# One product of sums for both halves of a pair, and an earlier list for the second pair, in an attention and MoE kernel

## Chip, cores and metric

The kernel runs on one core of a Trainium2 chip. The metric is device time in microseconds (us), the median of the runs; lower is better. Three runs of the kernel before gave 986.38, 987.79 and 989.44 us; the profiled execution has a span of 986.2 us.

## The reference

Routed attention, then a feed-forward block. Each query and each key is assigned to the nearest of 16 centroids of its head; a query sees only the keys of its own cluster.

```python
# q, k, v: (4, 8, 768, 64); centroids: (8, 16, 64)
mask = q_assign[:, :, :, None] == k_assign[:, :, None, :]
scores = where(mask, scale * (q @ k.T), -1e9)
attn = exp(scores - max); attn = attn / (sum(attn) + 1e-9)
x = (attn @ v) as (3072, 512)
h = x @ w_in                      # 512 x 2048
out = (h - tanh(h)) @ w_out       # 2048 x 512
```

## The kernel before

The 32 heads are taken as 16 pairs of heads: pair `n` is batch `n // 4`, heads `2 * (n % 4)` and the one after. The 768 queries of a pair are taken in two halves of 384. One half of one pair takes three steps of two key chunks each. The first batch runs all first halves of its four pairs and then all second halves (steps 0 to 23); every later pair runs half 0 and then half 1, six steps in a row.

In a step TensorE makes the scores of the step that follows (`begin`, line 451), with keys on the partitions, and the values product of the present step (`value`, line 505); ScalarE takes the exponential (473). VectorE multiplies it by the mask (`select`, line 483: row code equals key code) for each of the two key chunks and two heads, four operations a step. For most halves GpSimd adds the masked exponentials over the chunks into a tile `sum` (lines 492 and 496), so that only one product with ones is left at the end of a half: `total`, lines 532 to 553. It makes two products of 64 columns (line 539), one for each head, and ScalarE copies them out (544). For the first halves of the first batch TensorE accumulates the sums itself in four products of 32 columns a step (`sum_up`, line 520).

What follows depends on the pair. Where the result is needed soon (`soon(n)`: the last pair of each batch, and pair 2), VectorE takes reciprocals of the whole tile (603) and scales `xT` (606). Otherwise the sums travel by memory, since each is repeated on 64 partitions: `total` writes one row of each head to a list in DRAM (553), `compact` reads the list back spread over 128 partitions, six numbers each (566), `invert` takes the reciprocal on VectorE (575) and writes it back (577), `spread_out` reads it broadcast to 64 partitions a head (582), and `scale` multiplies (588). These five stages are put in `later` at 0, 1, 2, 3 and 5 steps after the end of the half; for pair 1's first half the last three come a step later (`slow`, line 1110).

Beside the attention steps runs the feed-forward block of the batch before: plain products for the first batch (lines 626 and 642), and for the others a Strassen form with 7 products in place of 8 (`up_product`, line 818, and `down_product`, line 869). `strassen_items` and `plain_items` return pieces with a weight, and each step takes as many as are due. Inside a piece `between()` is called; it takes the next share of the list `todo`, whose entry `i` of `len(todo)` falls into slot `i * slots / len(todo)`. So the length of `todo` decides how late each entry is issued. All engines run in the order that this program writes. Buffers: two of `sum` and two of `den` in pool `sump`, two score tiles in PSUM (`ps_s`, also used by the transposes of line 332), and three tiles of `ps_f` for everything else.

Of the kernel before, what the change touches and what calls it, by code (L numbers as in the profile page):

```python
# [30 lines left out]
F32 = mybir.dt.float32  # L31
# [4 lines left out]
ALU = mybir.AluOpType  # L36
# [22 lines left out]
def kernel(  # L59
# [119 lines left out]
    def fast():  # L179
# [352 lines left out]
        def total(n: int, half: int):  # L532
# [17 lines left out]
            for i in range(parts):  # L550
                for h in range(2):
                    r = h * D + i * D // 2
                    nc.sync.dma_start(lists[n, half][i, h : h + 1], t[r : r + 1])

        lists, spots = {}, {}
# [2 lines left out]
            return pairs[n][1] == HP - 1 or n == HP - 2  # L560

        def compact(n: int, half: int):
            spots[n, half] = each[:, len(spots)]
            t = lists.pop((n, half))
            for i in range(t.shape[0]):
                nc.sync.dma_start(
                    other if i else spots[n, half],
                    t[i].rearrange("h n -> (h n)").rearrange("(p i) -> p i", p=P),
                )

        def invert(n: int, half: int):
            t = spots[n, half]
            if summed(n, half):
                nc.vector.tensor_tensor(out=t, in0=t, in1=other, op=ALU.add)
            nc.vector.reciprocal(out=t, in_=t)
            back = lists[n, half] = dram.tile([2, TB], F32, name="back")
            nc.sync.dma_start(back.rearrange("h n -> (h n)").rearrange("(p i) -> p i", p=P), t)

        def spread_out(n: int, half: int):
            back = lists.pop((n, half))  # L580
            for h in range(2):
                nc.sync.dma_start(
                    dens[n, half][h * D : h * D + D], back[h : h + 1].to_broadcast([D, TB])
                )

        def scale(n: int, half: int):
            x = xT[n][:, half]
            nc.vector.tensor_tensor(out=x, in0=x, in1=dens.pop((n, half)), op=ALU.mult)

        tallies, picks = {}, []  # L590

# [157 lines left out]
        def open_stream():  # L749
            first_in.close()  # L750
            late_pools["stream"] = cx.enter_context(
                tc.tile_pool(name="stream_late", bufs=3, side="right", reuse_waits="tile")
            )
            for n in range(2):
                fetch_factors(n)
# [294 lines left out]
        for at, (n, half, s) in enumerate(steps):  # L1050
            b, p = pairs[n]
            following = steps[at + 1] if at + 1 < len(steps) else None
            if at == 4 * HALF:
                open_late()
            if at == 4 * HALF - 9:
                open_stream()
            if at in fills:
                fill, over = fills[at][0](), fills[at][1]
                whole, spent, since = sum(it[0] for it in fill), 0.0, at
            if at == 2 * HALF:  # L1060
                makers = [it for i in range(2) for it in up_maker(i)]
                makers += [it for i in range(2) for it in down_maker(i)]
            now = []
            part = (at - since + 1) / over
            while fill and (spent + fill[0][0] / 2 <= whole * part or part == 1):
                now.append(fill.pop(0))
                spent += now[-1][0]
            stages = ready.get(at, {})

            values_first = 1 in stages and not summed(n, half)  # L1070
            if values_first:
                value(n, half, s)
            if 1 in stages:
                stages[1]()

            for ahead, known in ((2, False), (5, True)):
                to = steps[at + ahead] if at + ahead < len(steps) else None
                if to and to[2] == 0 and (to[0] < HP and to[1] == 1) == known:
                    if not masked(*to[:2]):
                        spread(*to[:2])  # L1080
            if following and at >= NS - 1:
                begin(following)
            while picks:
                picks.pop(0)()
            share = paces.get(at, 0)
            todays, rounding = rounding[:share], rounding[share:]
            taken = s == NS - 1 and summed(n, half)
            if not taken:
                for piece in todays[:2]:
                    rest_of(piece)  # L1090
            if not values_first:
                value(n, half, s)
            if summed(n, half):
                if 0 in stages:
                    stages.pop(0)()
                sum_up(n, half, s)
            if s == NS - 1:
                take(n, half)
                if taken:
                    if soon(n):  # L1100
                        total(n, half)
                    for piece in todays[:2]:
                        rest_of(piece)
                if soon(n):
                    if summed(n, half):
                        picks.append(lambda n=n, half=half: pick(n, half))
                    divides = [lambda n=n, half=half, i=i: divide(n, half, i) for i in range(HCH)]
                else:

                    slow = int((n, half) == (1, 0))  # L1110
                    for i, stage in (
                        (0, total), (1, compact), (2 + slow, invert), (3 + slow, spread_out),
                        (5 + slow, scale),
                    ):
                        later.setdefault(at + i, []).append(
                            (i, lambda stage=stage, n=n, half=half: stage(n, half))
                        )

                if p == HP - 1 and (half == 1 or b == 0):
                    if summed(n, half):  # L1120
                        picks += divides
                    else:
                        total(n, half)
                        late += divides
                    divides = []
                if (n, half) == (HP - 1, 0):
                    load(HP)
                if half == 1:
                    load(n + (HP if n < 2 else 2), (2,) if n < 2 or n >= HP else ())

            todo = []
            if following:
                todo += [lambda i=i: select(*following[:2], 2 * following[2] + i) for i in range(2)]
            todo += [stages[i] for i in (5, 3, 4, 2) if i in stages]
            todo += late
            late = []
            if divides:
                if not taken:
                    todo.append(lambda n=n, half=half: total(n, half))
                late, divides = divides, []  # L1140

            for it in later.pop(at, []):
                if it[0] == 0:
                    todo.append(it[1])
                else:
                    listed.append(it[1])
            for i, piece in enumerate(todays):
                todo.append(lambda piece=piece: round_piece(piece))
                if i == 0:
                    todo += [lambda piece=piece: rest_of(piece) for piece in todays[2:]]  # L1150
            todo += listed
            listed = []

            light = [i for i in range(at, 4 * HALF - 2) if i % 3 and i % 6 != 1]
            if makers and at in light:
                share = -(-len(makers) // len(light))
                todo += makers[:share]
                del makers[:share]
            if "raw" in late_pools:
                todo += [check_done, check_done, check_on, check_on]  # L1160
                if p == HP - 1 and half == 1 and s == NS - 2:
                    todo += [lambda b=b, c=c: right_factors(b, c) for c in range(CH - 1)]
            slots = max(sum(it[1] for it in now), 1)
            place = iter(range(slots))
            turned_at = max(slots - 1 - now[-1][1], 0) if now else 0

            def between():
                i = next(place)
                for it in todo[i * len(todo) // slots : (i + 1) * len(todo) // slots]:
                    it()  # L1170

                if i == turned_at and 0 in stages:
                    stages[0]()

            if at in fills and "raw" in late_pools:
                for c in range(CH - 1 if at > 4 * HALF else 0, CH):
                    right_factors(b - 1, c)
            for it in now:
                it[2](between)
            if not now:  # L1180
                between()
# [225 lines left out]
```

## Time and profile before

| view | value |
|---|---|
| time, median of 3 | 987.79 us |
| span of the profiled execution | 986.2 us |
| line 539, products of the sums | 112 records, 22.8 us busy |
| line 520, the same with 32 columns | 96 records, 10.2 us busy |
| line 544, copy of a sum | 32, 491 ns each |
| line 496, add to a sum on GpSimd | 112, 1841 ns each |
| line 575, reciprocal of a list | 22, 184 ns each |
| line 588, scale | 22, mean 974 ns, median 556 ns |
| HBM traffic | 133 GB/s over the span |

A product in float32 appears in the trace as two records of TensorE, so one `total` is four records. A record is shown with its full latency (486 ns for 384 columns of moving data) while the next has long begun, so times of one record can't be added: the distance between starts is what TensorE spends. The chain of the page is followed back from the last instruction, and names at each step the work that released it.

### The profile page before, as it was taken

The page shows a single profiled execution, that of the slowest core. Times are in us where ns is not written, and L with a number is a line of the kernel's source. Part 1 is how long each engine was busy: PE and PEld are TensorE (multiplying, and loading weights), DVE is VectorE, ACT ScalarE, POOL GpSimd, SP SyncE. Part 2 cuts the span into 40 slices and gives each one's busy share as a digit, 9 for nine tenths or more (in the row PEclk, how much of TensorE's full clock was granted, in tenths as well). Part 3 has the DMA queues.
Part 4 walks back from the last instruction along what each step waited for, and adds up shares of the span by engine and source line. Part 5 has one row for each costly group of instructions (what it writes and reads, how often), then busy time and mean ns, then how long its engine had stood idle before and what let it go on. Part 6 is the DMA issues. An engine that isn't in the chain of part 4 may idle for free.

```text
span 986.2 us, 16627 instructions
## 1 busy us (share of the span) xinstructions
PE 976.0 (99%) x6456; PEld 464.9 (47%) x6456; DVE 531.0 (54%) x1019; ACT 321.5 (33%) x493; POOL 499.7 (51%) x347
## 2 busy tenths in 40 slices
PE   9999999999999999999999999999999999999997
PEld 5433443344443334444455555444455555444664
DVE  6457756447656567647554356655645336543011
ACT  5575554233333333243322222333341221122000
POOL 1025334445445454687676345666688345466600
PEclk9999999999999999999999999999999999999999
DMA  8755452025474723463635636344453232233221
GB/s 205 179 162 163 150 145 94 30 52 153 127 224 136 216 99 118 148 196 96 192 106 193 198 114 213 110 152 121 151 165 110 85 110 81 96 113 127 105 102 35
DMA packets 115977, 132.47 MB, mean 134 GB/s; under 512 B 62980, under 2 KB 95668, under 8 KB 113204
## 3 DMA queue, kind: packets, MB, share of 16 engines
q1 hardware_dynamic: 109508, 109.81, 37.0%
q0 software_dynamic: 6240, 21.50, 6.5%
q8 instruction: 53, 0.87, 0.4%
q14 instruction: 32, 0.26, 0.1%
q10 hardware_dynamic: 144, 0.03, 0.0%
HBM read 110.14 MB, written 21.17 MB: 133 GB/s over the span
## 4 chain that ended last, share of the span: by engine, by line
PE 94%; DVE 2%; DMA 2%; issue 1%; ACT 1%; SPq 0%; ACTq 0%; DVEq 0%
PE pd L869 22%; PE pu L818 22%; PE sc L451 13%; PE av L505 13%; PE o L642 8%; PE h L626 8%; PE pt L332 2%; PE den L539 2%; PE sim L351 1%; DMA den<-back 1%; PE pr L364 1%; DVE e L483 1%; PE den L520 0%; DMA back<-each 0%; PE pq L396 0%
## 5 line engine op out<-in xcount | busy, mean ns | idle before, releaser
L496 POOL TENSOR_TENSOR sum<-sum,e 128x768 f32<-128x768 f32 x112 | 206.2, 1841 | 105.2 <-DVE e L483 101.4
L483 DVE SCALAR_TENSOR_TENSOR e<-row,code,sc 128x384 f32<-128x384 bf16 x336 | 185.3, 608 | 94.9 <-ACT sc L473 72.1
L473 ACT ACTIVATE sc<-sc 128x768 f32<-128x768 f32 x168 | 125.9, 792 | 205.3 <-PE sc L451 187.6
L869 PE MATMUL pd<-stream,G 128*64 128x256 f32 x1728 | 191.8, 379 | 0.0
L869 PEld LDWEIGHTS pd<-stream,G 128*64 128x64 f32 x1728 | 123.7, 137 | 67.4 <-issue 7.9
L451 PE MATMUL sc<-t,t 64*128 64x384 f32 x768 | 150.2, 509 | 0.3 <-ACT e L473 0.3
L505 PE MATMUL av<-e,vals 128*64 128x384 f32 x768 | 145.6, 498 | 0.1
L813 POOL TENSOR_TENSOR G<-G,th 128x768 f32<-128x768 f32 (+1 forms) x51 | 88.0, 1736 | 98.6 <-ACT th L811 98.6
L818 PE MATMUL pu<-xT,stream 128*64 128x384 f32 x768 | 134.9, 488 | 0.7 <-DVE top L372 0.7
L818 PE MATMUL pu<-diff,stream 128*64 128x384 f32 x576 | 102.4, 487 | 0.0
L451 PEld LDWEIGHTS sc<-t,t 64*128 64x128 f32 x768 | 65.8, 186 | 74.5 <-issue 40.5
L492 POOL TENSOR_TENSOR sum<-e 128x768 f32<-128x768 f32 x28 | 56.8, 2030 | 80.1 <-DVE e L483 71.7
L626 PE MATMUL h<-xT,w_in 128*64 128x384 f32 x512 | 86.3, 487 | 1.0 <-DVE xT L606 1.0
L818 PEld LDWEIGHTS pu<-xT,stream 128*64 128x64 f32 x768 | 54.1, 137 | 69.6 <-issue 62.2
L642 PE MATMUL o<-w_out,g 128*64 128x512 f32 x384 | 86.4, 594 | 0.0
L505 PEld LDWEIGHTS av<-e,vals 128*64 128x64 f32 x768 | 47.6, 136 | 82.2 <-issue 80.0
L811 ACT ACTIVATE th<-G 128x768 f32<-128x768 f32 (+1 forms) x51 | 40.9, 806 | 123.1 <-DVE G L806 119.5
L818 PEld LDWEIGHTS pu<-diff,stream 128*64 128x64 f32 x576 | 40.8, 137 | 49.9 <-issue 45.2
L806 DVE TENSOR_TENSOR G<-pu,u 128x384 f32<-128x384 f32 x72 | 39.8, 553 | 41.8 <-PE pu L818 41.2
L626 PEld LDWEIGHTS h<-xT,w_in 128*64 128x64 f32 x512 | 36.4, 137 | 47.3 <-issue 45.2
L642 PEld LDWEIGHTS o<-w_out,g 128*64 128x64 f32 x384 | 27.0, 137 | 50.1 <-issue 49.4
L880 DVE SCALAR_TENSOR_TENSOR c<-pd,du 128x256 f32<-128x256 f32 x36 | 15.2, 421 | 62.7 <-PE pd L869 62.7
(127 smaller groups left out, 840.0 us busy)
## 6 DMA issues: line engine op xcount, KB each, us to landing
stream<-up_factors SPq DMA_DIRECT2D x24, 896.0 KB
stream<-down_factors SPq DMA_DIRECT2D x21, 1024.0 KB
raw<-in_moe_w_in_dram POOLq DMA_DIRECT2D x16, 512.0 KB, 5.0
raw<-in_moe_w_out_dram POOLq DMA_DIRECT2D x16, 512.0 KB, 4.4
again<-in_moe_w_in_dram SPq DMA_DIRECT2D x32, 256.0 KB
again<-in_moe_w_out_dram SPq DMA_DIRECT2D x32, 256.0 KB
x<-in_q_dram SPq DMA_DIRECT2D x32, 192.0 KB
x<-in_k_dram SPq DMA_DIRECT2D x32, 192.0 KB
```

What stands on the lines that cost most here:

```text
L451: nc.tensor.matmul(sc[i][:, h, 0:TB], lhsT=turned[n, 1][r].rearrange("p a n -> p (a n)")[:, j * P : (j + 1) * P], rhs=turned[n, 0][r, half ...
L473: nc.scalar.activation(out=out, in_=sc[i][:, :, 0:TB], func=ACT.Exp, scale=SCALE)
L483: nc.vector.scalar_tensor_tensor(out=e[:, h], in0=rows[n, half][:, h], scalar=codes[n][:, 1, j // HCH, h, j % HCH : j % HCH + 1], in1=sc[: ...
L492: nc.gpsimd.tensor_tensor(out=s, in0=pair[0], in1=pair[1], op=ALU.add)
L496: nc.gpsimd.tensor_tensor(out=s, in0=s, in1=pair[i], op=ALU.add)
L505: nc.tensor.matmul(avs[n, half][h * D : h * D + D], lhsT=vals[n][:, h, j], rhs=e[i][:, h], start=(j == 0), stop=(j == NCH - 1),)
L626: nc.tensor.matmul(h[r], lhsT=w_in[i][:, c, o * P : (o + 1) * P][:, r], rhs=xT[c][:, half], start=(c == 0), stop=(c == CD - 1),)
L642: nc.tensor.matmul(acc[sub][r], lhsT=gs[f % HF][:, f // HF, sub * P : (sub + 1) * P][:, r], rhs=w_out[f // FQ][:, f % FQ], start=(f == seq ...
L811: nc.scalar.activation(out=th, in_=t, func=ACT.Tanh)
L813: nc.gpsimd.tensor_tensor(out=t, in0=t, in1=th, op=ALU.subtract)
L818: nc.tensor.matmul(ps[r], lhsT=streams[base + i][:, c, k_, r], rhs=right[c], start=(c == 0), stop=(c == CH - 1),)
L869: nc.tensor.matmul(ps[r], lhsT=left(i)[:, r], rhs=t[:, i], start=(i == 0), stop=(i == HF - 1))
```

## The change

For a pair that is not `soon` and not in the first batch (`joined`), the sums of both halves are kept until the end of the second one. Then `total_both` makes four products of 32 columns, one for each half and head, into one PSUM tile; one copy, one list of four rows, one `compact` of 12 numbers a partition, one reciprocal and one list back follow. `spread_out` then fills two tiles: that of half 0 and a new one of half 1 (from a pool of its own, `den_late`, once that is open), and `scale` handles both halves. `total_both` is put at index 1 of `todo`, ahead of the `select` that starts the next pair's sum. The stages of half 0 fall away for these pairs. Apart from that, `slow` is removed: the stages of pair 1's first half come at 2, 3 and 5 steps like those of all others. Its purpose is to spend fewer instructions and transfers on the sums, and to have the second pair's scale early.

```diff
+        def joined(n: int):
+            return n >= HP and not soon(n)
+
+        def total_both(n: int):
+            ps = ps_f.tile([P, TB], F32, name="den", tag="f")
+            for half in range(2):
+                t = sums.pop((n, half))
+                for h in range(2):
+                    r = half * D + h * D // 2
+                    nc.tensor.matmul(
+                        ps[r : r + D // 2], lhsT=ones[:, 0 : D // 2], rhs=t[:, h], start=True,
+                        stop=True, tile_position=(0, r),
+                    )
+            t = dens[n, 0] = sump.tile([P, TB], F32, name="den")
+            nc.scalar.activation(out=t, in_=ps, func=ACT.Copy, bias=EPS / words)
+            lists[n, 1] = dram.tile([2, 2, TB], F32, name="list2")
+            for half in range(2):
+                for h in range(2):
+                    r = half * D + h * D // 2
+                    nc.sync.dma_start(lists[n, 1][half, h : h + 1], t[r : r + 1])
...
         def compact(n: int, half: int):
+            t = lists.pop((n, half))
+            if joined(n):
+                for i in range(2):
+                    spots[n, i] = each[:, len(spots)]
+                nc.sync.dma_start(
+                    each[:, len(spots) - 2 : len(spots)].rearrange("p a b -> p (a b)"),
+                    t.rearrange("a h n -> (a h n)").rearrange("(p i) -> p i", p=P),
+                )
+                return
...
         def invert(n: int, half: int):
+            if joined(n):
+                at = list(spots).index((n, 0))
+                t = each[:, at : at + 2].rearrange("p a b -> p (a b)")
+                nc.vector.reciprocal(out=t, in_=t)
+                back = lists[n, half] = dram.tile([2, 2, TB], F32, name="back2")
...
+                return
...
         def spread_out(n: int, half: int):
             back = lists.pop((n, half))
+            if joined(n):
+                pool = late_pools.get("den", sump)
+                dens[n, 1] = pool.tile([P, TB], F32, name="den")
+                for i in range(2):
+                    for h in range(2):
+                        nc.sync.dma_start(
+                            dens[n, i][h * D : h * D + D], back[i, h : h + 1].to_broadcast([D, TB])
+                        )
+                return
...
         def scale(n: int, half: int):
-            x = xT[n][:, half]
-            nc.vector.tensor_tensor(out=x, in0=x, in1=dens.pop((n, half)), op=ALU.mult)
+            for i in (0, 1) if joined(n) else (half,):
+                x = xT[n][:, i]
+                nc.vector.tensor_tensor(out=x, in0=x, in1=dens.pop((n, i)), op=ALU.mult)
...
+            late_pools["den"] = cx.enter_context(
+                tc.tile_pool(name="den_late", bufs=1, side="right", reuse_waits="tile")
+            )
...
-                else:
-
-                    slow = int((n, half) == (1, 0))
-                    for i, stage in (
-                        (0, total), (1, compact), (2 + slow, invert), (3 + slow, spread_out),
-                        (5 + slow, scale),
-                    ):
+                elif half == 1 or not joined(n):
+                    for i, stage in ((0, total), (1, compact), (2, invert), (3, spread_out), (5, scale)):
+                        if i == 0 and joined(n):
+                            continue
...
                 todo += [lambda i=i: select(*following[:2], 2 * following[2] + i) for i in range(2)]
+
+                if half == 1 and s == NS - 1 and joined(n):
+                    todo.insert(1, lambda n=n: total_both(n))
```

More of the change, by code (lines that the diff above doesn't have):

```diff
@@ L562, in compact @@
         def compact(n: int, half: int):
+            t = lists.pop((n, half))
[7 more added lines that the diff above has]
+                return
             spots[n, half] = each[:, len(spots)]
-            t = lists.pop((n, half))
             for i in range(t.shape[0]):
@@ L571, in invert @@
         def invert(n: int, half: int):
+            if joined(n):
[4 more added lines that the diff above has]
+                nc.sync.dma_start(
+                    back.rearrange("a h n -> (a h n)").rearrange("(p i) -> p i", p=P), t
+                )
+                return
             t = spots[n, half]
@@ L580, in spread_out @@
             back = lists.pop((n, half))
+            if joined(n):
[3 more added lines that the diff above has]
+                    for h in range(2):
+                        nc.sync.dma_start(
+                            dens[n, i][h * D : h * D + D], back[i, h : h + 1].to_broadcast([D, TB])
+                        )
+                return
             for h in range(2):
@@ L752, in open_stream @@
                 tc.tile_pool(name="stream_late", bufs=3, side="right", reuse_waits="tile")
+            )
+            late_pools["den"] = cx.enter_context(
+                tc.tile_pool(name="den_late", bufs=1, side="right", reuse_waits="tile")
             )
```

## The prediction

> **What bounds the kernel now.** I read the page's busy times first, then its chain by line, then the timeline of TensorE around every product of a sum.
>
> ```profile
> PE 976.0 (99%) x6456; PEld 464.9 (47%) x6456; DVE 531.0 (54%) x1019; ACT 321.5 (33%) x493; POOL 499.7 (51%) x347
> PE 94%; DVE 2%; DMA 2%; issue 1%; ACT 1%; SPq 0%; ACTq 0%; DVEq 0%
> ```
>
> TensorE is busy for 976.0 of 986.2 us and carries 94% of the chain; the other engines are at half or less. By stretches (busy time in windows) it is idle 1.7 us in 24 to 83 us, 0.0 in 83 to 376, 0.3 in 376 to 610, 0.3 in 610 to 835. So after 83 us a microsecond taken from TensorE is a microsecond of the end, unless a new wait takes its place; ScalarE, VectorE and DMA work saved there is worth nothing by itself. The products of the sums, line 539, hold 1.8% of the chain: 17.8 us for 28 calls.
>
> ```profile
> 425.76 0.81 PE L539 MATMUL den<-sum,ones 128*64 128x384 f32 x4
> 426.40 1.78 PE L818 MATMUL pu<-diff,stream 128*64 128x384 f32 x10
> 243.53 0.81 PE L539 MATMUL den<-sum,ones 128*64 128x384 f32 x4
> 244.28 1.53 PE L332 MATMUL pt<-ident,x 128*128 128x128 f32 x12
> ```
>
> Columns: start, time, engine, line, operation, tiles, shape, count. What an entry costs TensorE is the distance to the next start, since ends overlap. One `total` (two products of 64 columns, four records) costs 0.64 us between products of the same width, and 0.75 before full-width work. The extra 0.10 belongs to the change of width: products of line 626 pay the same before line 451 (232.86 to 238.12 is 5.26 for 32 records, 5.16 without it).
>
> ```profile
> 27.70 1.51 PE L505 MATMUL av<-e,vals 128*64 128x384 f32 x8
> 29.14 0.85 PE L520 MATMUL den<-e,ones 128*32 128x384 f32 x8
> 29.92 0.33 PE L364 MATMUL pr<-ident,simt 128*128 128x128 f32 x1
> 225.80 1.51 PE L505 MATMUL av<-e,vals 128*64 128x384 f32 x8
> 227.14 2.75 PE L626 MATMUL h<-xT,w_in 128*64 128x384 f32 x16
> ```
>
> This is the kernel's own example of what the change adds: line 520 already makes four products of 32 columns with ones. They cost 0.78 us before full-width work, and 0.67 before other products of 32 columns (25.92 to 26.59). The eight `av` records cost 1.44 ahead of them, but 1.34 ahead of 64-column work: entering the 32-column tiling costs 0.10.
>
> **What the Trainium skill says.** "TensorEngine Tiling (Array Packing)", section Tiling Modes: 128 rows can be split in two tiles of 64 columns or four of 32, tiles work in parallel, and changing the mode, not just the tile, drains the engine. The trace agrees: four products of 32 columns take 0.67 us and two of 64 take 0.64, and a mode change costs about 0.10. "DMA: Bandwidth & Descriptors", section Anatomy of one DMA, puts about 2 us of fixed cost on a DMA, mostly the write receipt, with the wait on the issuing queue. Here the write of `back` at 68.12 is released 4.50 us later, longer under load. "GPSIMD Engine Reference", section Specifications: GpSimd's SBUF interfaces are shared with VectorE, in contention with instructions of two SBUF inputs. Line 588, which is one, takes 547 to 2140 ns, median 556; at 77.73 it took 1.91 us beside a GpSimd add.
>
> **The change, part by part.** A pair is joined when n is 4 or more and `soon(n)` is false: 4, 5, 6, 8, 9, 10, 12, 13, 14, nine pairs.
>
> Removed from TensorE: the first half's `total`, nine times. By the order of instructions it just disappears, and its neighbours close up. Each is 0.645 us: 9 x 0.645 = 5.80 us. Where full-width scores followed, the mode change remains, because the products before pay it.
>
> Put in place of the second half's `total`: four products of 32 columns, at the same places in TensorE's order. For n = 4, 5, 6, 10 transposes follow and for 14 scores: 0.10 to enter + 0.78, in place of 0.75, adds 0.13 each, 5 x 0.13 = 0.65. For n = 8, 9, 12, 13 there are 64-column products on both sides: 0.10 to enter + 0.67 + the exit to 64 columns, which the trace does not show cleanly. I bound it by 0 and by the 0.11 of the exit to full width, and take 0.08: 0.85 for 0.65 adds 0.20 each, 4 x 0.20 = 0.80. Together 1.45; by bounds of the exit 1.1 to 1.6, and up to 2.3 if every entry costs a second 0.10. Net on TensorE: 5.80 - 1.45 = 4.35 us less.
>
> Hidden: nine evictions of 0.49 us on ScalarE, nine small reciprocals of 0.18 on VectorE, and fewer DMAs (10 for 12 per pair; reads and writes of 48-byte runs for 24). ScalarE and VectorE have half their time free, and TensorE waits for none of these.
>
> New waits. First, both halves' sums live until `total_both`, so with two buffers the next pair's first add (line 492, GpSimd) must wait for it. Behind that add stand the next `sum` adds and, in the later stages, the tanh subtractions. At the boundary near 244 it starts at 243.94 in the trace of before, against an end of the products near 244.6: a delay of 0.7, with 4.5 us of GpSimd idle after it. In the up-product stages it starts 2.5 to 3.8 us after the products anyway. Second, the products themselves wait for the pair's last add:
>
> ```profile
> 713.99 3.71 POOL L496 TENSOR_TENSOR sum<-sum,e 128x768 f32<-128x768 f32 x2
> 718.75 0.81 PE L539 MATMUL den<-sum,ones 128*64 128x384 f32 x4
> ```
>
> The add ended at 717.70, so 1.05 us are spare. Over the nine places the slack is 6.6, 6.4, 7.6, 1.4, 2.9, 9.2, 1.4, 1.05 and 9.2 us. If it runs out, everything on TensorE waits, so this is the place to look for a loss; but the add depends on TensorE's own earlier work, which does not get slower.
>
> Moved: with fewer items per step, the second half of a `select` (two of four line 483 operations) falls one slot later in VectorE's order in some steps, behind one addition of an up or down product. The scores of the next step need both score buffers free. The nearest: at 417.76 to 418.89 two `e` move behind the addition at 418.81. That addition's product ends near 417.9, so the two would end near 419.5, against scores at 420.35. That is 0.85 us of slack in place of 1.46. The others I looked at keep 0.8 or more. I cost it at nothing, hidden by TensorE's own products.
>
> Pair 1's first half: its lists are inverted, written back and scaled a step sooner.
>
> ```profile
> 67.91 0.20 DVE each L575
> 68.12 4.50 DMA back<-each
> 73.13 4.50 DMA den<-back
> 77.73 0.71 DVE xT L588
> 79.56 2.58 DVE den L603 x3
> 82.16 0.57 DVE xT L606
> ```
>
> This is a piece of the chain (start, us, what). VectorE's scale waits for the DMA until 77.66; behind it stand the reciprocals of pair 2 (line 603) and its scale (606), for which TensorE waits: its products would go on at 81.56 and do so at 82.78, 1.22 us late. In the new order the inversion follows the scale of pair 0, which ends at 63.97. The lists were asked for at 59.16 and 59.72, so they should have landed. `back` leaves near 64.4, is released near 68.9, and the den broadcast lands near 73.5, or 75.3 if it takes the 6.41 us of the first one. The scale now stands ahead of four `e` operations, where VectorE is free at 74.33. These are 0.57 later then; the second score tile waits for them and so does TensorE (77.50 becomes about 78.1). The tally products end near 78.9, three reciprocals take 2.57, the scale 0.57: 82.1 in place of 82.73. I take 0.6 us off; 1.2 if nothing else shifts, and 0.2 lost if the broadcast lands at 75.3.
>
> Sum: 5.80 - 1.45 + 0.60 = 4.95; 987.79 - 4.95 = 982.8 us.
>
> **Rivals.** (a) A new wait takes back half: the delayed `e` or the 1.05 to 1.4 us slacks give out. Two of the four products between 64-column work waiting 1.2 us make 2.4, which leaves 985.2. For it: slack under 1 us in several steps. Against: the line 539 products never wait for sums now, and VectorE and GpSimd run in step with TensorE. (b) Slower: at the three places with least slack a GpSimd pair of adds (3.7 us) slips entirely ahead of the products, 3 x 3.7 = 11.1 less 4.95: 993.9. For it: the held buffers, and GpSimd adds lasting up to 4.2 us. Against: GpSimd was idle 6.05 us before the adds of that step. (c) The lists are hidden anyway and the tile changes cost 2.3: the start gains nothing, 987.79 - 5.80 + 2.3 = 984.3. (d) Better: start 1.2 and the changes of width 1.1: 987.79 - 5.80 + 1.1 - 1.2 = 981.9.
>
> **How the numbers follow.** The main case 0.55, (d) 0.10, (c) 0.15, (a) 0.12, (b) 0.08. Main, (c) and (d) lie beyond 0.3% (984.8); (a) is within it; (b) is slower: 0.80, 0.12 and 0.08. The range takes in (d) less 1 us, since three runs of one kernel span 986.38 to 989.44, and (a) with a little: 980.8 to 985.6; (b) and some of the edges are left out.
>
> **What would show it.** The profile after should have 9 entries of four 32-column products, each 0.65 to 0.8 to the next start with 0.10 more ahead of it; 40 of the 112 records of line 539 left, and 72 narrow ones of the new line; VectorE's scale of pair 1 near 74.4 and the gap at 82.78 mostly gone; no TensorE wait on GpSimd or on `e` after 83 us; stretches after 83 us shorter by about 4.3 in sum. The prediction is wrong if such waits appear, if the 32-column products take two turns (1.3 us), or if the lists land late and VectorE stalls at 64.

## The result, and the profile after

| | runs | median, us | range, us | span of the profiled execution |
|---|---|---|---|---|
| before | 6 | 988.12 | 986.38 to 989.44 | 986.2 |
| after | 6 | 983.03 | 982.07 to 983.24 | 981.3 |

The ratio of the times is 0.9949, with a 95% interval of 0.9937 to 0.9962: the changed kernel is faster by 5 us in 988. The forecast was 982.8 us.

The profile page of the kernel after, busy times and the chain by engine:

```profile
PE 972.3 (99%) x6456; PEld 461.1 (47%) x6456; DVE 534.5 (54%) x1010; ACT 316.6 (32%) x484; POOL 498.8 (51%) x347
PE 97%; DVE 1%; DMA 0%; issue 0%; SPq 0%; ACT 0%; DVEq 0%
```

TensorE lost 3.7 us of busy time, and its count of instructions stayed at 6456: 72 records of two 64-column products became 72 records of four 32-column ones, which overlap. DMA and VectorE have fallen from 4% to 1% of the chain, all of it in the first 90 us. A share of the chain is not a price: some 23 us of the chain moved there to TensorE, and the start got about 1 us shorter.

**The sums.** Lines have moved: the joined products are line 566, the old ones still 539; the up products are now line 871. Two groups of the list of TensorE's groups by lines (count | busy us, mean ns | idle before):

```profile
L539 PE MATMUL den<-sum,ones 128*64 128x384 f32 x40 | 8.2, 486 | 0.0
L566 PE MATMUL den<-sum,ones 128*32 128x384 f32 x72 | 7.7, 498 | 0.0
```

And the timeline of TensorE (start, us, engine, line) around the two places that the prediction shows of the kernel before. First two more lines of before, which stand on either side of its single `total`, then the kernel after:

```profile
424.47 1.46 PE L818 MATMUL pu<-xT,stream 128*64 128x384 f32 x8
...
429.09 1.53 PE L332 MATMUL pt<-ident,x 128*128 128x128 f32 x12
```

```profile
421.26 1.46 PE L871 MATMUL pu<-xT,stream 128*64 128x384 f32 x8
422.65 0.85 PE L566 MATMUL den<-sum,ones 128*32 128x384 f32 x8
423.44 2.80 PE L871 MATMUL pu<-diff,stream 128*64 128x384 f32 x16
426.17 1.09 PE L332 MATMUL pt<-ident,x 128*128 128x128 f32 x8
...
241.95 0.85 PE L566 MATMUL den<-sum,ones 128*32 128x384 f32 x8
242.73 1.53 PE L332 MATMUL pt<-ident,x 128*128 128x128 f32 x12
```

Read the distances between starts. The joined group takes 0.79 us (422.65 to 423.44) where one half's `total` took 0.64. The eight records ahead of it take 1.39 (421.26 to 422.65) instead of 1.29 (424.47 to 425.76), and the sixteen after it 2.73 (423.44 to 426.17) instead of 2.69 (426.40 to 429.09). So between 64-column products the joined group costs 0.10 + 0.15 + 0.04 = 0.29 us more than the single `total`. Before transposes (241.95 to 242.73) it takes 0.78 for 0.75.

**The start.** Lines have moved here too: the scale is line 638, the inversion 615, the reciprocals and the scale of pair 3 653 and 656 (before: 588, 575, 603 and 606). VectorE and then TensorE of the kernel after, and last the line of before where TensorE stopped:

```profile
64.14 0.19 DVE L615 RECIPROCAL each<-each 128x6 f32<-128x6 f32 x1
73.89 0.55 DVE L638 TENSOR_TENSOR xT<-xT,den 128x384 f32<-128x384 f32 x1
74.36 2.18 DVE L483 SCALAR_TENSOR_TENSOR e<-row,code,sc 128x384 f32<-128x384 bf16 x4
78.51 2.58 DVE L653 RECIPROCAL den<-tally 128x128 f32<-128x128 f32 x3 [1.97 <-PE tally L648]
81.12 0.56 DVE L656 TENSOR_TENSOR xT<-xT,den 128x384 f32<-128x384 f32 x1
```

```profile
77.53 0.86 PE L648 MATMUL tally<-den,firsts 64*64 64x384 f32 x4
78.32 1.51 PE L505 MATMUL av<-e,vals 128*64 128x384 f32 x8
79.66 4.55 PE L676 MATMUL h<-xT,w_in 128*64 128x384 f32 x26
```

```profile
82.78 6.03 PE L626 MATMUL h<-xT,w_in 128*64 128x384 f32 x36 [1.04 <-DVE xT L606]
```

The scale of pair 1 waits for no DMA any more. Pair 3's scale (line 656) ends at 81.68, before 82.73, and the products of line 676 run through from 79.66, where the kernel before stopped until 82.78. The DMA queue of SyncE shows how the lists fared:

```profile
64.36 0.32 SPq L617 DMA_DIRECT2D back<-each  x1
65.76 1.09 SPq L631 DMA_DIRECT2D den<-back  x2
```

`back` is issued at 64.36 and the broadcast that waits for it at 65.76: 1.40 us, where the same pair was 4.52 us apart (68.12 and 72.64) in the kernel before.

**Where the 5 us lie.** The values products (`av`, line 505) come in the same order in both traces. I subtracted the start of each in the trace after from the start of the same one in the trace before; the difference grows where something was saved and falls where something was lost. Gains and losses here come from starts in ns, so they can differ by 0.01 from the rounded starts.

| start before, us | start after, us | gained so far | what happened since the row above |
|---|---|---|---|
| 78.29 | 78.32 | -0.03 | no net change: 0.6 lost at 22 us, 0.8 regained at 60 us, 0.2 lost at 76 us |
| 90.22 | 89.19 | 1.04 | the stop at 82.78 is gone: +1.07 |
| 225.80 | 224.12 | 1.68 | first half's `total` of pair 4 gone: +0.65 |
| 245.74 | 244.19 | 1.54 | joined group of pair 4, before transposes: -0.14 |
| 404.01 | 400.80 | 3.21 | pairs 5 and 6, and first half of pair 8 |
| 431.88 | 428.97 | 2.92 | joined group of pair 8, between 64 columns: -0.29 |
| 781.50 | 776.50 | 5.00 | pairs 9 to 14 |

All nine removed halves give 0.64 or 0.65, 5.81 us together. The joined groups cost 0.14 at five places (pairs 4, 5, 6, 10, 14) and 0.29 at four (pairs 8, 9, 12, 13), 1.84 together. The start gives 1.07. TensorE's idle time between 24 and 83 us fell further, from 1.69 to 0.16 us, but that includes a wait of 0.61 for `hot` at 60 us; it is 0.56 in two more traces of the changed kernel.

**The new waits.** GpSimd's first add of a pair (line 492) does wait for the joined products now; GpSimd's list by lines, and TensorE's waits (waits us, times, longest):

```profile
L492 POOL TENSOR_TENSOR sum<-e 128x768 f32<-128x768 f32 x28 | 55.5, 1983 | 77.9 <-DVE e L483 42.2 <-PE den L566 35.7
```

```profile
PE pu L871 <- DVE top L372: 0.7, 2, 0.3
PE av L505 <- DVE e L483: 0.4, 1, 0.4
```

The 35.7 us are five waits of GpSimd, up to 7.6 us long. No wait of TensorE for GpSimd is in its list. The two stops of 0.3 us for line 372 are in the kernel before too; the 0.4 us lies at 22 us. So after 83 us the change has put no new wait on TensorE.

### The profile page after: what moved, and what is told of

The parts are those of the page before. It is cut to its first block, busy times and chain, and to the rows that moved or that the text cites. A ratio compares the mean times of both kernels' runs of the same rounds, so it can differ in the third digit from the quotient of the medians.

```text
span 981.3 us, 16550 instructions
## 1 busy us (share of the span) xinstructions
PE 972.3 (99%) x6456; PEld 461.1 (47%) x6456; DVE 534.5 (54%) x1010; ACT 316.6 (32%) x484; POOL 498.8 (51%) x347
## 4 chain that ended last, share of the span: by engine, by line
PE 97%; DVE 1%; DMA 0%; issue 0%; SPq 0%; ACT 0%; DVEq 0%
PE pd L922 22%; PE pu L871 22%; PE sc L451 14%; PE av L505 14%; PE o L692 8%; PE h L676 8%; PE pt L332 2%; PE sim L351 1%; PE den L520 1%; PE warm L302 1%; PE den L566 1%; PE den L539 1%; PE pr L364 1%; DVE e L483 1%; DMA row<-q_codes 0%; PE pq L396 0%
```

## The experiments

All times are medians, beside the kernel before run on the same chip. A stands for the theory of the prediction: the removed products on TensorE pay 4 us, the earlier list about 1, independently. B, for the first two, has the microsecond at the start be only the scatter of the start between two executions, so that the earlier list pays nothing; C, for the two kernels after those, has the saving come from fewer transfers, waits for lists and small operations instead of the products. Where a gain or loss at one place is given, it is read from one trace of each kernel.

### Each part alone

First the joined sums alone: the changed kernel with pair 1's lists back at their old step.

```diff
+slow = int((n, half) == (1, 0))
-for i, stage in ((0, total), (1, compact), (2, invert), (3, spread_out), (5, scale)):
+for i, stage in (
+    (0, total), (1, compact), (2 + slow, invert), (3 + slow, spread_out),
+    (5 + slow, scale),
+):
```

> The changed kernel with the second pair's lists put back to their old, later steps; the joined sums stay. Theory A (TensorE's own sequence sets the end: nine removed products of 0.645 us less the changes of width, 3.9 us by the traces; and about 1.0 us from the second pair's lists at the start): 988.1 - 3.9 = 984.2 us, ratio 0.996, and the products of line 676 stop again for about 1 us near 82 us, waiting for VectorE's scale. Theory B (the microsecond at the start is only the scatter of the start between two runs): 983.1 us, no stop near 82.

Measured 983.98 us (982.04 to 984.56), before 988.52; ratio 0.9946, 0.9933 to 0.9960. The stop at 82.8 is back, in TensorE and in the chain of waits (start, us, what):

```profile
79.77 2.10 PE L676 MATMUL h<-xT,w_in 128*64 128x384 f32 x12
82.81 1.51 PE L676 MATMUL h<-xT,w_in 128*64 128x384 f32 x8 [0.93 <-DVE xT L656]
```

```profile
68.26 4.49 DMA back<-each
...
73.25 5.53 DMA den<-back
```

By the same subtraction as above, the start gives 0.10 in place of 1.07, and the rest from 90 us on 3.96, as in the changed kernel (5.00 - 1.04). So the 1.07 us belong to the earlier list, and the joined sums give 4.0 without it. The range of the times takes in both forecasts; the trace decides for A.

Then the other part alone, the kernel before with `slow` at zero:

```diff
-slow = int((n, half) == (1, 0))
+slow = 0
```

> The kernel before with only the second pair's lists a step sooner. Theory A: 988.1 - 1.0 = 987.1 us, ratio 0.999, no stop of the products of line 626 near 82 us. Theory B: 988.1 us, the same as before.

Measured 988.22 us (986.63 to 991.03, 13 runs), before 988.52; ratio 0.9993, 0.9985 to 1.0002. The interval takes in no change (B) and A's 0.999 alike, so the time decides nothing. The trace does: the stop at 82.8 is gone and gives 1.07, so B falls, but 0.63 of it is lost again near 329, which A did not expect. TensorE and VectorE there:

```profile
329.52 0.84 PE L332 MATMUL pt<-ident,x 128*128 128x128 f32 x6 [0.19 <-issue]
330.57 0.84 PE L332 MATMUL pt<-ident,x 128*128 128x128 f32 x6 [0.20 <-issue]
```

```profile
328.28 2.19 DVE L483 SCALAR_TENSOR_TENSOR e<-row,code,sc 128x384 f32<-128x384 bf16 x4 [2.34 <-DMA row<-q_codes]
```

VectorE's masks wait 2.34 us for the row codes of the next pair (1.89 in the kernel before), and the transposes, which use the score tiles that the masks free, come late. To see whether it matters that the scale itself moved too, I left it at its old step and moved only the inversion and the broadcast:

```diff
-    (0, total), (1, compact), (2 + slow, invert), (3 + slow, spread_out),
+    (0, total), (1, compact), (2, invert), (3, spread_out),
     (5 + slow, scale),
```

> The kernel before with only the second pair's inversion, write-back and broadcast a step sooner; its scale stays behind the four mask operations where it was. If the gain at the start comes from the lists having landed: 987.1 us as in the list-only run, and the scale starts near 76.5 us in place of 77.7. If it comes from the scale's place ahead of the mask operations: 988.1 us, no gain.

Measured 987.69 us (986.57 to 988.44, 13 runs), before 988.13; ratio 0.9996, 0.9988 to 1.0004: again both forecasts lie inside. The start gives 1.07 again in the trace, with the scale after the four masks; and 0.60 is lost at the same place, for the same wait. VectorE:

```profile
76.13 0.55 DVE L588 TENSOR_TENSOR xT<-xT,den 128x384 f32<-128x384 f32 x1
...
327.06 2.19 DVE L483 SCALAR_TENSOR_TENSOR e<-row,code,sc 128x384 f32<-128x384 bf16 x4 [2.42 <-DMA row<-q_codes]
```

So it is the list's landing that frees the start, not the place of the scale. The new place even costs something. With the scale ahead of them the masks begin 6.70 us after the first of the three reciprocals that VectorE takes near 68 us (changed kernel, and list alone), and 6.24 us after it with the scale behind them (here, and in the kernel before); TensorE's tally follows the masks by 3.17 or 3.18 in all four. The changed kernel with the scale left in its old place was not run.

For the loss near 329, here is SyncE's queue in the kernel before, and then in the kernel after:

```profile
313.12 2.21 SPq L745 DMA_DIRECT2D stream<-up_factors  x2
316.48 0.31 SPq L402 DMA_DIRECT2D q_codes<-qc  x1
316.83 0.39 SPq L566 DMA_DIRECT2D each<-list  x1
323.71 0.32 SPq L409 DMA_DIRECT2D row<-q_codes  x1
```

```profile
308.11 2.03 SPq L795 DMA_DIRECT2D stream<-up_factors  x2
313.78 0.31 SPq L402 DMA_DIRECT2D q_codes<-qc  x1
318.09 0.33 SPq L409 DMA_DIRECT2D row<-q_codes  x1
```

The read of the row codes is issued 7.2 us after their write in the kernel before and 4.3 us after it in the kernel after; in the two kernels with the earlier list alone it is 7.9 and 8.0. By its list of waits, SyncE waits there for the landing of the write itself: 6.4 us before, 7.0 and 7.2 with the earlier list alone, 3.9 after. The reading of a first half's list that stands between them takes SyncE 0.39 us, so its place in the queue is not what is waited for. The DMA engines are full at that time (0.93 to 0.99 of ten us in all four), with the two stream reads of 896 KB. Where lists are joined, these begin 5.7 us ahead of the write instead of 3.4, and in the kernel before a first half's list write, for whose sum SyncE waits 4.2 us, stands in the queue ahead of them. That this list is what delays the codes is argued and was not separated. Why the landing takes 0.6 to 0.8 longer when only the start is earlier stays open: stream reads and write lie 3.36 us apart there as before.

### Which part of the joining pays

The lists joined as in the changed kernel, but with the old products: two of 64 columns for each half, in two PSUM tiles with two copies, at the place of the joined group.

```diff
 for half in range(2):
+    ps = ps_f.tile([P, TB], F32, name="den", tag="f")
...
-            ps[r : r + D // 2], lhsT=ones[:, 0 : D // 2], rhs=t[:, h], start=True,
-            stop=True, tile_position=(0, r),
+            ps[h * D : h * D + D], lhsT=ones, rhs=s[:, h], start=True, stop=True
...
+    t = dens[n, half] = (pool if half else sump).tile([P, TB], F32, name="den")
+    nc.scalar.activation(out=t, in_=ps, func=ACT.Copy, bias=EPS / words)
```

> The changed kernel with one list for both halves as there, but its sums made at the same place by four products of 64 columns in two PSUM tiles and copied by two operations of ScalarE: all joined transfers and reciprocals stay, only TensorE's work is as before. Theory A: the 5.8 us of the removed first halves come back as 9 x 0.645 at the ends of the pairs, without changes of width; only the start's 1.0 us stays: 987.1 us, ratio 0.999. Theory C (the gain comes from fewer transfers, list waits and small operations): 983 to 984 us.

Measured 988.11 us (987.62 to 988.78), before 988.52; ratio 0.9995, 0.9986 to 1.0003. C falls for the transfers: saved alone, they bring nothing that can be seen. (This kernel makes two copies on ScalarE again; the next one keeps the single copy.) Each first half gives 0.64 and each second half takes 0.64 back; the start gives 1.07, and there is no loss near 329. At two places more is lost than A expected, 0.37 near 483 (pair 9) and 0.64 near 718 (pair 13). TensorE:

```profile
717.71 1.46 PE L567 MATMUL den<-sum,ones 128*64 128x384 f32 x8
719.59 1.51 PE L865 MATMUL pu<-diff,stream 128*64 128x384 f32 x8 [0.42 <-DVE u L853]
```

The product waits for VectorE's addition `u`, which reads an earlier up product and ends at 719.53. In the changed kernel the product at this place, at 714.86, does not wait for that addition, which begins at 715.23. The two groups of sums take two of the three `ps_f` tiles, so I take it that the next up product must reuse a tile one product too soon; no run isolates this. It would make the single tile part of what the narrow form saves at such places.

Then the price of one set of narrow products, by making them twice, same inputs and outputs:

```diff
+kept.append((r, t, h))
...
+for r, t, h in kept:
+    nc.tensor.matmul(ps[r : r + D // 2], lhsT=ones[:, 0 : D // 2], rhs=t[:, h], start=True,
+                     stop=True, tile_position=(0, r))
```

> The changed kernel with the four products of each joined pair made twice into the same tile (same values). Theory A: 9 x 0.65 = 5.9 us more than the changed kernel: 988.9 us, and the group in the trace takes 1.43 us to the next start in place of 0.78. Theory C: TensorE's products are not what the gain is made of: 983 to 984 us.

Measured 988.81 us (987.72 to 989.60), before 988.52; ratio 1.0002, 0.9994 to 1.0010. Against the changed kernel's 983.03, from another set of runs, this is 5.78 us for nine sets, 0.64 each; from 90 us on the two traces differ by 5.80. TensorE:

```profile
422.65 1.46 PE L878 MATMUL pu<-xT,stream 128*64 128x384 f32 x8
424.04 0.85 PE L567 MATMUL den<-sum,ones 128*32 128x384 f32 x8
424.71 0.83 PE L573 MATMUL den<-sum,ones 128*32 128x384 f32 x8
425.47 2.80 PE L878 MATMUL pu<-diff,stream 128*64 128x384 f32 x16
```

The first set takes 0.67 to the next start and the second 0.76, where the single set took 0.79: what a set costs beside 32-column work is 0.64 to 0.67, the rest is paid once for entering and leaving the width. The second sets cost more than the 3.96 that the joining gains, though one copy and one list a pair are kept: the gain is TensorE's time, and C falls for the copies too.

### The changed kernel again

> The changed kernel itself, as the reference for the two runs beside it: 983.0 us, ratio 0.995.

> The changed kernel once more as the reference beside it: 982.9 us.

Measured 982.72 (982.24 to 983.58) and 982.93 us (982.58 to 983.08), ratios 0.9945 and 0.9947: the same in two other sets of runs.

### Without the changes of width

If the 1.84 us are what the change of width costs, they must go when the joined group stands beside work of its own width. The kernel has such work: `similar`, line 351, four products of 32 columns, comes once in every pair. I moved the joined group behind it (the last pair's stays, having no next), and GpSimd's first add of the next pair with it, since it must follow the products.

```diff
 if half == 1 and s == NS - 1 and joined(n):
-    todo.insert(1, lambda n=n: total_both(n))
+    if n + 2 < len(pairs):
+        owed.append(lambda n=n: total_both(n))
+    else:
+        todo.insert(1, lambda n=n: total_both(n))
...
 if 1 in stages:
     stages[1]()
+while owed:
+    owed.pop(0)()
```

> The changed kernel with the four products of a joined pair moved from between work of other widths to directly behind the four 32-column products of `similar` (line 351) at the start of the next step, for eight of the nine pairs; the next pair's first add of sums on GpSimd is issued behind them. Theory A with changes of width as the cost (0.14 a place before full-width work, 0.29 between 64-column products): the group should cost about 0.67 us with none of these: 4 x 0.12 + 4 x 0.26 = 1.5 us less, 981.5 us, 0.9985 of the changed kernel. Rival: the extra 0.14 and 0.29 are not changes of width but belong to four products in one tile, or the later list and add make a new wait: 983.0 us or more.

Measured 983.15 us (982.17 to 984.04), before 988.13; ratio 0.9951, 0.9938 to 0.9965: no better than the changed kernel beside it (982.72), where 981.5 was expected. The mechanism was there all the same: every moved group costs 0.64 or 0.65. But two stops came with it, at pairs 9 and 13. TensorE at both:

```profile
482.39 0.84 PE L332 MATMUL pt<-ident,x 128*128 128x128 f32 x6 [0.48 <-DVE e L483]
...
715.46 0.85 PE L332 MATMUL pt<-ident,x 128*128 128x128 f32 x6 [0.71 <-DVE e L483]
```

There the transposes follow closely, and without the sums ahead of them they reach the score tiles before VectorE's masks have freed them (at pair 9 the last two masks run from 481.12, behind an addition of an up product that begins at 480.65). So the group was, at those two places, time in which VectorE caught up. The next kernel leaves these two where the change has them:

```diff
-    if n + 2 < len(pairs):
+    if n + 2 < len(pairs) and n not in (9, 13):
```

> As the run beside `similar`, but the products of pairs 9 and 13 stay where the change put them. In that run the width changes were gone at all places, and at these two alone the transposes stopped 0.48 and 0.71 us for VectorE's masks, so that it gained almost nothing. If that is the whole account, six places gain 4 x 0.14 + 2 x 0.29 = 1.1 us with no stop: 981.8 us, span by 1.1 us shorter than the changed kernel's at equal starts. Rival: the stops come with any later list or add: stops at other places, 982.7 us or more.

Measured 981.14 us (980.97 to 982.43), before 988.22; ratio 0.9932, 0.9918 to 0.9946. In the same set of runs the changed kernel had 982.93. After 83 us only the two old stops of 0.3 us are left. TensorE:

```profile
427.67 1.46 PE L511 MATMUL av<-e,vals 128*64 128x384 f32 x8
429.06 0.85 PE L351 MATMUL sim<-t,bd 128*32 128x384 f32 x8
429.73 0.83 PE L572 MATMUL den<-sum,ones 128*32 128x384 f32 x8
430.49 0.92 PE L451 MATMUL sc<-t,t 64*128 64x384 f32 x4
```

`similar` takes the 0.10 of entering ahead of it, as it always did (427.67 to 429.06 is 1.39), and the change back to full width comes at the end (0.76), as it always did. The joined group in between adds 0.64 to 0.65 by the subtraction. From 90 us on this kernel gains 5.10 over the kernel before, the changed kernel 3.96: 1.14 of the 1.84 us were to be had, as expected. The medians differ by more, 1.8 us; the traces don't show where the rest comes from.

## Why the prediction was right, point by point

Forecast 982.8, measured 983.03. The mechanism held. Two terms of the sum were mis-sized in opposite directions, and that their errors cancel is luck.

**Removed products: right.** 9 x 0.645 = 5.80 was forecast, and 5.81 is what the nine places show. That TensorE's time after 83 us becomes the end's time one to one is confirmed by the kernel that made the products twice: nine times 0.64 added, 5.78 longer. The stretches after 83 us were to shrink by 4.35 in sum, and did by 3.96.

**Changes of width: too low, 1.84 for 1.45.** At the five places before full-width work 0.13 was forecast and 0.14 measured. The miss is in the four between 64-column products, 0.29 for 0.20. The step that failed is "the exit to 64 columns, which the trace does not show cleanly", bounded by 0.11 and taken as 0.08. With the entry of 0.10 and the group's 0.67 taken out, it is 0.79 + 0.04 - 0.67 = 0.16. The weight loads of the kernel after (PEld, idle before each) show something of it:

```profile
421.91 0.14 PEld L871 LDWEIGHTS pu<-xT,stream 128*64 128x64 f32 x2 [0.18 <-issue]
422.65 0.16 PEld L566 LDWEIGHTS den<-sum,ones 128*32 128x32 f32 x8 [0.60 <-issue]
423.43 0.20 PEld L871 LDWEIGHTS pu<-diff,stream 128*64 128x64 f32 x4 [0.62 <-DVE e L483]
```

Within one width a weight load begins every 0.32 us here, one group ahead of its products. At both changes of width it begins with the products themselves (422.65, 423.43), after 0.60 and 0.62 us of idleness: nothing is loaded ahead across the change. VectorE, named at 423.43, is not the reason: at pairs 9 and 13 the same 0.60 and 0.62 stand with no engine waited for. The Trainium skill, "TensorEngine Tiling (Array Packing)", section Tiling Modes, says that a change of mode drains TensorE; the trace agrees, and the price here is about 0.10 to enter and 0.16 to leave for 64 columns. My upper case of 2.3 for all nine contained it; the range by the bounds of the exit, 1.1 to 1.6, did not.

**The start: too low, 1.07 for 0.6.** The 0.57 by which the scale puts off the four masks was said to push TensorE's tally from 77.50 to 78.1. The scale does put them off, by 0.46 (they begin 6.70 us after the first reciprocal near 68 us, where it was 6.24). But that reciprocal begins 0.43 sooner, at 67.65 for 68.08, for the most part since the inversion, now done at 64.14, no longer stands ahead of it; with the joined sums alone, where it still does, it begins at 68.22. So the masks begin at 74.36 (before 74.33) and the tally at 77.53. The prediction counted what comes ahead of the masks and put at nothing what goes away there. The scale that TensorE waits for ended 1.05 earlier, close to the upper value of 1.2. It is pair 3's, not pair 2's as the prediction says: its tally at 77.50 follows pair 3's last sums, at 74.91. The receipt of `back` was also taken wrongly, as 4.5 us from the trace of before, and took 1.4, so that the broadcast was issued at 65.76 instead of 68.9; this cost the sum nothing, since the main case had the broadcast landed in time. The errors of 0.39 and 0.47 nearly cancel: 5.81 - 1.84 + 1.07 - 0.03 (the first 78 us) is 5.0, against 4.95.

**New waits: right.** The first add waits for the joined products, at five places for up to 7.6 us, and no one on TensorE waits for it. The joined products themselves never waited for the sums; at pair 13 the add ended at 713.07 and they began at 714.07, 1.0 us later, where 1.05 was read from the trace of before. Two of the slacks listed were misread: the trace of before has 1.06 at pair 9, not 2.9, and 5.5 at pair 6, not 7.6. Pair 9 thus had as little room as pair 13, and had 0.99 after; it held. Of the moved `e` no trace is to be seen in TensorE's waits, so rivals (a) and (b) fall. How much room was left is another question: taking the group from its place at pairs 9 and 13 made TensorE wait 0.48 and 0.71 us for `e`. A third buffer of sums, which would take the wait of line 492 away, wasn't tried.

**Fewer transfers are worth nothing: right alone, wrong in company.** The kernel with joined lists and wide products shows that they bring nothing measurable by themselves. But the earlier list kept only 0.4 of its 1.07 us with the old lists, by the one trace of each of the two kernels, and all of it with the joined ones. The prediction added the two parts as if they were independent; by the traces they are 3.96 + 0.10 and 1.07 - 0.63 apart, and 5.0 together. It looked for slack only where the change touches the order, and not at the landing of the row codes. That the joined lists leave room there is in none of its terms, so this part of the agreement is luck too.

**Rival (c)** had the start gain nothing and the width cost 2.3; the start gave 1.07 and the width cost 1.84. **Rival (d)** was near with the start (1.2) and wrong with the width (1.1).

## What to carry to other kernels

Where TensorE carries 94% of the chain, count the distances between starts of its products, not the busy time, and price a narrow group by its neighbours: set beside work of the same width it costs only its own time. Before taking time out of the bound engine, look also for transfers that land with little to spare, row codes here: they need not come earlier along with it. Where an operation moves in an engine's order, count what leaves the place as well as what comes. And a group that is moved away may have been the time another engine needed to catch up, so move it place by place.

## What the runs showed of the hardware beyond that

Four products of 32 columns and two of 64, both with 128 rows and a moving side of 384 float32 columns, cost the same: 0.64 to 0.67 against 0.64 us. A change to 32 columns and back costs 0.14 more than a wide group at the same place where full-width work follows, 0.29 between 64-column products, and nothing beside other 32-column products. A write of 3 KB and its receipt took 1.40 us (64.36, after) and 4.52 us (68.12, before), from its issue to that of the transfer that waits for it. The DMA engines were busy 0.19 of the first time and 0.60 of the second; that this is the reason was not separated. "DMA: Bandwidth & Descriptors" of the Trainium skill, section Anatomy of one DMA, gives about 2 us of fixed cost for DMAs that GpSimd issues; these two are issued by SyncE and lie on either side of it, and no run here issues the same write from GpSimd.
